# States of batches 2 and 3 turned by TensorE products instead of a transposing transfer, with a new order of the head

## The chip, the cores and the metric

The kernel runs on 1 core of one Trainium2 chip. The metric is device time in microseconds of one execution; times of several runs are given by their median. A profiled execution carries its own time and the span of its instructions.

## The reference

Eight batches of eight heads: a cross attention between 512 tokens `x` and 32 state rows of each head, in both directions, then a two-layer network with a leaky relu over all 8 x 544 rows.

```python
B, H, S, Ns, D = (8, 8, 512, 32, 64)
scores = scale * np.matmul(x, state.transpose(0, 1, 3, 2))     # softmax over the 32 states
xread = np.matmul(a, state)
scores2 = scale * np.matmul(state, x.transpose(0, 1, 3, 2))    # softmax over the 512 tokens
sread = np.matmul(a2, x)
attn = np.concatenate([xread, sread], axis=2)                  # [B, H, 544, 64]
...
h = x @ w_in          # x: attn as [4352, 512]; w_in [512, 2048]
g = np.maximum(0.01 * h, h)
return (g @ w_out)    # w_out [2048, 512]
```

## The kernel before, in words

**Work on a batch.** The kernel never forms `xread`. For each batch it multiplies the scaled states with the rows of `w_in` of their head (`a_m`, L383 to L397), which gives `M`, 256 rows (8 heads x 32 states, as two groups of 128) by 2048; the first layer is then `M` times the probabilities `aT` (`ff1`, L410, for batch 0 `Quad`, L1035), and ScalarE applies the leaky relu on the way out of PSUM (`hT`). The second layer multiplies `hT` with `w_out`: for batch 0 plainly (`piece`), for the others with seven products in place of eight on halves (`Fast`, `Batch`), whose sums of operands VectorE and GpSimd make. The scores (`a_scores`, L221) are products of the states with the transposed x (`xT`). Softmax over states runs on VectorE with 32x32 block operations: `a_top` (`mrow`, L235), `a_rows` (`mrowb`, L243), `a_less` (`sh`, L248), `a_exp` on ScalarE (L255), `a_probs` (L260 to L274, ends in `aT`). The softmax over tokens is `a_max2` (`mcol`, L307) and two exponentials on ScalarE (`a_exp2`, L313).

**What states need.** As left operand of both products a state must stand with D on the partitions: `st_of` (L214) gives 64 rows by 32 columns of a head. For batches 0 and 1 `state01` (L157) makes this: one load of 128 rows of 1 KB (`st0f`, partition p holds four rows of state), a scaling to bf16 (L864), eight products of its 64-column pieces with columns of an identity (L161), and two copies out of PSUM that put the four rows back into order (L165, L169). For batches 2 and 3, and for 4 to 7, `load_state` (L177) makes eight loads into 32 partitions each, `state_t` (L186) scales on GpSimd (L187) and issues a transposing transfer on the SP queue (L188) from `stb` to `st_t`.

**Order.** Every engine's order is written out by hand: the program calls the helpers one after the other, and each engine runs its own calls in that order. Names of the first stretch, the head: `spin` are products without use that keep TensorE going while x loads; `x0_t` transposes batch 0's x on TensorE, `xt0_evict` copies it out; `scores0`/`max0` give the maxima of batch 0 in two halves u of the tokens; `rows0` puts the scores in rows; `split0` splits the negated maximum into two bf16 parts `hi`, `lo`, which `spread0` adds to the scores by products; `exp0`, `sum0`, `recip0`, `probs0` finish the softmax. Loads of weights are issued by GpSimd, x of batch 0 by SP and ScalarE. Batch 1's products (`ff`), batch 2's `M` and scores and the pieces of batch 0's second layer are then mixed by hand, up to a `stretch` of batch 2 whose order is a string, `FIRST`; batches 3 on use `ORDER`. The memset at L1088 touches two columns of `stf`, so that the loads of batches 2 and 3 (SP, L181) come no earlier than it. PSUM is shared by tags: `sc` holds one tile, in turn the scores and some of the `pm` tiles; `ph` and `py` hold two each; `big` one.

Of the kernel before, what the change touches and what calls it, by code (L numbers as in the profile page):

```python
# [9 lines left out]
P = 128  # L10
B, H, S, D = 8, 8, 512, 64
# [19 lines left out]
def kernel(  # L31
# [41 lines left out]
    idle = consts.tile([P, S], BF16, name="idle")  # L73
    nc.vector.memset(idle[:], 0.0)
# [57 lines left out]
    def load_w_out(c, parts=1):  # L132
        n = 4 // parts
        for j in range(4 * c, 4 * (c + 1), n):
            nc.gpsimd.dma_start(
                w_out_bf[:, j:j + n, :],
                moe_w_out[P * j:P * (j + n), :].rearrange("(j p) f -> p j f", p=P),
            )

    def spin(n, tag):  # L140
        p = psum.tile([P, S], FP32, name="pspin", tag=tag, bufs=2 if tag in ("ph", "py") else 1)
        for _ in range(n):
            nc.tensor.matmul(p[:], lhsT=idle[:, :P], rhs=idle[:], start=True, stop=True)
# [30 lines left out]
    stf = [consts.tile([P, hi - lo, P], FP32, name=f"stf{lo}", tag=f"stf{lo}") for lo, hi in groups]  # L174
    stb = [consts.tile([P, hi - lo, P], BF16, name=f"stb{lo}") for lo, hi in groups]
# [689 lines left out]
    spin(7, "py")  # L865
    state01()
    spin(3, "py")


    pxt = {}  # L870

    def x0_t(u, k):
        b = k // 3
        if (u, b) not in pxt:
            pxt[u, b] = psum.tile([P, 3 - 2 * b, 2, P], BF16, name="pxth", tag=("ph", "py")[u])
        for v in range(2):
            nc.tensor.transpose(
                pxt[u, b][:, k % 3, v, :],
                a0.xb[:, 2 * u + v, 2 * k:2 * k + 2, :].rearrange("p h d -> p (h d)"), ident[:],
            )  # L880
# [31 lines left out]
    def spread0(dst, parts, start):  # L912
        for i, part in enumerate(parts):
            for q in range(2):
                for v in range(2):
                    for c in range(NK):
                        n = H * v + NK * q + c
                        nc.tensor.matmul(
                            dst[NS * c:NS * (c + 1), q, P * v:P * (v + 1)],
                            lhsT=part[:, n:n + 1].to_broadcast([P, NS]),  # L920
                            rhs=ident[:], start=start, stop=start or (q == v == i == 1),
                        )
# [8 lines left out]

    def split0(m, eng):
        hi = att.tile([P, NG], BF16, name="hi0", tag="hi0")
        VEC(hi[:], m[:])
        lo = att.tile([P, NG], BF16, name="lo0", tag="lo0")
        with nc.allow_low_precision(reason="the second of two parts of one fp32 value"):
            eng.tensor_tensor(out=lo[:], in0=m[:], in1=hi[:], op=ALU.subtract)
        return hi, lo
# [19 lines left out]
    def recip0(u):  # L958
        q = att.tile([P, NG], BF16, name="q0", tag="q0")
        with nc.allow_low_precision(reason="one rounding, of the finished reciprocal"):  # L960
            nc.vector.reciprocal(q[:], r0[u][:])
        return q

    def recip0_rows(u, q):
        qb0[u] = psum.tile([P, 2, HT], FP32, name="qb0", tag="ph")
        spread0(qb0[u], (q,), True)
# [6 lines left out]
    for c in range(3):  # L973
        load_w_in(c)
    cast_x0(0, 0, NT, VEC)
    for k in (1, 2):
        cast_x0(k, 0, 2, VEC)
    for k in (1, 2):
        cast_x0(k, 2, NT, VEC)
    cast_x0(3, 0, 2, VEC)  # L980
    cast_x0(3, 2, NT, POO)
    for u, k in ((0, 0), (1, 0), (0, 1), (0, 2), (1, 1), (1, 2), (0, 3), (1, 3)):
        x0_t(u, k)
    for u in range(2):
        xt0_evict(u, 0, SCA)
        xt0_evict(u, 1, VEC)
# [3 lines left out]
    for v in range(2):  # L990
        scores0(0, v)
        max0(0, v)
    m = split0(m0[0], nc.gpsimd)
    load_w_in(3)
    load_w_out(0)
    for u in range(2):
        nc.gpsimd.dma_start(
            a1.xb[:, NK * u:NK * (u + 1)].rearrange("p h t d -> p h (t d)"),
            x[1, NK * u:NK * (u + 1)].rearrange("h (p t) d -> p h (t d)", t=NT),
        )  # L1000
    load_w_out(1, 2)
    load_w_out(2)
    for h in (0, NK):
        load_x(2, nc.gpsimd, h, h + NK)
    load_w_out(3, 2)
    rows0(0)
    scores0(1, 0)
    max0(1, 0)
    rows0(1)
    spread0(scn[0], m, False)  # L1010
    exp0(0)
    scores0(1, 1)
    max0(1, 1)
    for u in range(2):
        eps0(u)
    pm = a_m(a0, 0, "big")
    SCA(a0.M[:, 0, :DM], pm[:, 0, :])
    sum0(0)
    m = split0(m0[1], nc.vector)
    q = recip0(0)  # L1020
    spread0(scn[1], m, False)
    exp0(1)
    recip0_rows(0, q)
    VEC(a0.M[:, 1, :DM], pm[:, 1, :])
    probs0(0)
    pm1 = a_m(a1, 0, "sc")
    sum0(1)
    q = recip0(1)
    pm = a_m(a0, 1, "big")
    for g in range(2):  # L1030
        SCA(a0.M[:, g, DM:2 * DM], pm[:, g, :])
# [33 lines left out]
    def m0_evict(c, pm):  # L1065
        for d in range(DM * c, DM * (c + 1), 2 * P):
            VEC(a0.M[:, :, d:d + 2 * P], pm[:, :, d - DM * c:d - DM * c + 2 * P])

    first = Quad(0, 0, "py")
    first.product(range(2))  # L1070
    recip0_rows(1, q)
    probs0(1)
    m_evict(a1, 0, pm1, VEC)
    first.product(range(2, 4))
    first.relu()
    for u, j, tag in (
        (0, 4, "ph"), (1, 0, "big"), (1, 4, "py"), (0, 8, "ph"), (1, 8, "py"), (0, 12, "ph"), (1, 12, "big"),
    ):
        quad = Quad(u, j, tag)
        quad.product()  # L1080
        quad.relu()
        if (u, j) == (1, 0):
            m0_evict(2, a_m(a0, 2, "sc"))
        if (u, j) == (0, 8):
            pm = a_m(a0, 3, "big")
            a_scores(a0)
            m0_evict(3, pm)
            nc.vector.memset(stf[0][:, 0, D - 1:D + 1], 0.0)  # L1088
            a_max2(a0)
# [12 lines left out]
    def m_make(a, c, tag):  # L1102
        pmt[a.b, c] = a_m(a, c, tag)
# [10 lines left out]
    piece(0, h0, 1, 0)  # L1114
    piece(0, h0, 0, 0)
    a_exp2(a0, 0)
    turn(0)
    open_xb(2)
    weights_open()
    wide = psum.tile([P, 2, DM], FP32, name="pyw", tag="big", bufs=1)  # L1120
    VEC(a1.xT[:, :, 0:2, :], pt[0][:])
    turn(1)
    a_exp2(a0, 1)
    piece(0, h0, 2, 0, bank=wide[:, 0])
    VEC(a1.xT[:, :, 2:4, :], pt[1][:])
    load_state(0)
    m_make(a1, 1, "ph")
    a_scores(a1)
    piece(0, h0, 2, 1, copy=None, part=(0, 1))
    m_take(a1, 1, 0, SCA)  # L1130
    piece(0, h0, 0, 1, copy=None, part=(0, 1))
    piece(0, h0, 3, 0, bank=wide[:, 1])
    piece(0, h0, 2, 1, copy=None, part=(2, 3))
    weights_sum(0, 0, 4, nc.gpsimd)
    m_make(a1, 2, "ph")
    piece(0, h0, 3, 1, copy=None, part=(0, 1))
    piece(0, h0, 1, 1, copy=None, part=(0, 1))
    weights_sum(2, 0, 4, nc.gpsimd)
    a_open(a2, 2)
    m_take(a1, 1, 1, VEC)  # L1140
    m_take(a1, 2, 0, SCA)
    piece(0, h0, 3, 1, copy=None, part=(2, 3))
    piece(0, h0, 3, 2, copy=None, part=(0, 1))
    piece(0, h0, 2, 2, copy=None, part=(0, 1))
    a_top(a1)
    state_t(0)
    a_rows(a1)
    a_less(a1)
    a_exp(a1)
    m_take(a1, 2, 1, SCA)  # L1150
    cast_x(2, 0, 4, SCA)
    cast_x(2, 4, 5, POO)
    cast_x(2, 5, 6, POO)
    cast_x(2, 6, 7, POO)
    a_max2(a1)
    a_probs(a1, 0)
    a_probs(a1, 1)
    cast_x(2, 7, 8, POO)
    weights_sum(2, 4, 8)
    a_xt_dma(a2, slice(1, 2))  # L1160
    weights_sum(1, 4, 8)
    weights_sum(3, 4, 8, nc.gpsimd)
    a_exp2(a1, 0)
    weights_sum(1, 0, 4, nc.gpsimd)
    weights_sum(0, 4, 8, nc.gpsimd)
# [3 lines left out]
    piece(0, h0, 2, 2, copy=None, part=(2, 3))  # L1169
    piece(0, h0, 0, 1, copy=None, part=(2, 3))  # L1170
    cast_x(3, 0, 2, POO)
    a_exp2(a1, 1)
    piece(0, h0, 3, 2, copy=None, part=(2, 3))
    piece(0, h0, 0, 2, copy=None, part=(0, 1))
    piece(0, h0, 1, 1, copy=None, part=(2, 3))
    piece(0, h0, 1, 2, copy=None, part=(0, 1))
    piece(0, h0, 1, 2, copy=None, part=(2, 3))
    piece(0, h0, 0, 2, copy=None, part=(2, 3))
    m_make(a1, 3, "ph")
    cast_x(3, 2, 4, POO)  # L1180
    m_take(a1, 3, 0, SCA)
    m_make(a2, 0, "sc")
    m_take(a1, 3, 1, SCA)
    piece(0, h0, 3, 3, copy=None, part=(0, 1))
    ff(0)
    m_take(a2, 0, 0, SCA)
    relu.pop(0)()
    piece(0, h0, 2, 3, copy=None, part=(0, 1))
    piece(0, h0, 3, 3, copy=None, part=(2, 3))
    ff(1)  # L1190
    relu.pop(1)()
    piece(0, h0, 0, 3, copy=None, part=(0, 1))
    piece(0, h0, 2, 3, copy=None, part=(2, 3))
    ff(2)
    m_take(a2, 0, 1, VEC)
    cast_x(3, 4, 6, POO)
    ff(3)
    a_scores(a2)
    y_store(0, 2, VEC)
    a_top(a2)  # L1200
    a_a2t(a0)
    a_rows(a2)
    relu.pop(2)()
    relu.pop(3)()
    y_store(0, 3, SCA)
    ff(4)
    cast_x(3, 6, 8, POO)
    relu.pop(4)()
    piece(0, h0, 0, 3, copy=None, part=(2, 3))
    ff(5)  # L1210
    ff(6, "big")
    a_open(att_of[3], 3)
    a_less(a2)
    piece(0, h0, 1, 3, copy=None, part=(0, 1))
    ff(8)
    y_store(0, 0, SCA)
    relu.pop(5)()
    relu.pop(6)()
    a_max2(a2)
    piece(0, h0, 1, 3, copy=None, part=(2, 3))  # L1220
    y_store(0, 1, VEC)
    before.run(1)
    ff(10, "big")
    relu.pop(8)()
    a_exp(a2)
    a_xt_dma(att_of[3])
    load_state(1, range(0, 2))
    a_a2t(a1)
# [349 lines left out]
```

## Time and profile before

| What | Value |
|---|---|
| median of 3 runs | 201.35 us (201.06 to 201.36) |
| the profiled execution, its own time | 201.61 us |
| its span | 199.8 us |
| granted TensorE clock, mean | 0.998 |
| TensorE / VectorE / ScalarE / GpSimd busy | 193.8 / 164.8 / 150.1 / 63.9 us |
| transposing transfer of the states of batches 2 and 3, issue to landing | 4.4 us |

The table is read against the span: an engine whose busy time is near it has little to give, and what matters is where that engine waits. The profile's rows give starts in us from the span's start. PE is TensorE's products, PEld its weight loads, DVE is VectorE, ACT ScalarE, POOL GpSimd, SP SyncE, which here only issues transfers.

### The profile page before, as it was taken

The page shows a single profiled execution, that of the slowest core. Times are in us where ns is not written, and L with a number is a line of the kernel's source. Part 1 is how long each engine was busy: PE and PEld are TensorE (multiplying, and loading weights), DVE is VectorE, ACT ScalarE, POOL GpSimd, SP SyncE. Part 2 cuts the span into 40 slices and gives each one's busy share as a digit, 9 for nine tenths or more (in the row PEclk, how much of TensorE's full clock was granted, in tenths as well). Part 3 has the DMA queues.
Part 4 walks back from the last instruction along what each step waited for, and adds up shares of the span by engine and source line. Part 5 has one row for each costly group of instructions (what it writes and reads, how often), then busy time and mean ns, then how long its engine had stood idle before and what let it go on. Part 6 is the DMA issues. An engine that isn't in the chain of part 4 may idle for free.

```text
span 199.8 us, 5151 instructions
## 1 busy us (share of the span) xinstructions
PE 193.8 (97%) x2106; PEld 136.5 (68%) x2106; DVE 164.8 (82%) x282; ACT 150.1 (75%) x286; POOL 63.9 (32%) x90
## 2 busy tenths in 40 slices
PE   7999998999999999999999999999999999999993
PEld 2566533446677667767777777777777788799882
DVE  2676498599999998997999899999899877995613
ACT  3478628599779649997899779996999768767710
POOL 8473284790009102720413040500050024005350
PEclk9999999999999999999999999999999999999999
DMA  6999997999571998398293614080013401310026
GB/s 203 212 207 192 199 292 136 206 318 162 101 220 27 197 276 165 58 255 268 51 259 113 184 22 85 3 262 0 3 51 159 82 3 76 134 56 0 5 82 182
DMA packets 40616, 27.50 MB, mean 138 GB/s; under 512 B 25424, under 2 KB 37840, under 8 KB 40592
## 3 DMA queue, kind: packets, MB, share of 16 engines
q1 hardware_dynamic: 34032, 20.35, 39.7%
q0 software_dynamic: 5728, 6.03, 16.8%
q10 hardware_dynamic: 832, 0.79, 1.2%
q8 instruction: 16, 0.26, 0.6%
q14 instruction: 8, 0.07, 0.1%
HBM read 17.30 MB, written 8.91 MB: 131 GB/s over the span
## 4 chain that ended last, share of the span: by engine, by line
PE 90%; DMA 4%; DVE 3%; POOL 0%; issue 0%; ACT 0%; ACTq 0%
PE yq L770 43%; PE ph L414 18%; PE pm L393 4%; PE pf L492 3%; PE yu L770 3%; PE pl L660 3%; PE ph L1051 3%; DMA st_t<-stb 2%; DMA xf<-in_x_dram 2%; PE py L699 2%; PE pl L581 2%; PE pyw L699 1%; PE psn L359 1%; PE sc L225 1%; PE php L1051 1%; PE phw L427 1%
## 5 line engine op out<-in xcount | busy, mean ns | idle before, releaser
L420 ACT ACTIVATE hT<-ph 128x512 bf16<-128x512 f32 x84 | 49.1, 608 | 14.3 <-PE ph L414 14.3
L770 PEld LDWEIGHTS <-su 128*128 128x128 bf16 x480 | 46.2, 98 | 12.4 <-ACT hT L420 0.4
L414 PE MATMUL ph<-aT,M 128*128 128x512 bf16 x168 | 47.9, 379 | 0.0
L770 PEld LDWEIGHTS <-hT 128*128 128x128 bf16 x336 | 32.3, 98 | 12.0 <-issue 2.7
L770 PE MATMUL yq<-tw_xf,su 128*128 128x256 bf16 x224 | 30.8, 273 | 0.0
L770 PE MATMUL yq<-w_out_bf,hT 128*128 128x256 bf16 x224 | 29.2, 273 | 0.0
L114 POOL CAST xb<-xl 128x512 bf16<-128x512 f32 (+1 forms) x24 | 15.2, 673 | 20.9 <-DMA xl<-in_x_dram 20.9
L414 PEld LDWEIGHTS <-M 128*128 128x128 bf16 x168 | 16.0, 98 | 7.7 <-issue 1.9
L759 DVE TENSOR_TENSOR su<-hT 128x1024 bf16<-128x1024 bf16 x28 | 19.1, 686 | 2.6 <-ACT hT L420 2.5
L842 POOL TENSOR_TENSOR yo<-sv,sv 128x512 f32<-128x512 f32 x7 | 9.3, 1330 | 37.2 <-ACT e L313 31.4
L1283 ACT CAST M<-pm 128x512 bf16<-128x512 f32 x30 | 16.8, 596 | 0.6 <-PE pm L393 0.6
L779 ACT COPY sv<-yq 128x512 f32<-128x512 f32 x24 | 14.0, 587 | 3.4 <-PE yq L770 3.3
L770 PE MATMUL yq<-tw_x,su 128*128 128x256 bf16 x112 | 16.3, 273 | 0.0
L770 PE MATMUL yq<-w_out_bf,su 128*128 128x256 bf16 x112 | 15.3, 273 | 0.0
L782 DVE TENSOR_TENSOR yo<-yq,sv 128x512 f32<-128x512 f32 x20 | 13.5, 677 | 2.1 <-PE yq L770 2.1
L770 PE MATMUL yq<-tw_x,hT 128*128 128x256 bf16 x104 | 13.9, 273 | 0.0
L313 ACT ACTIVATE e<-sc,mcol 128x512 bf16<-128x512 f32 x16 | 11.2, 704 | 0.2 <-DVE mcol L307 0.2
L699 PEld LDWEIGHTS <-hT 128*128 128x128 bf16 x64 | 5.9, 98 | 7.4 <-issue 0.9
L759 DVE TENSOR_TENSOR su<-su,hT 128x1024 bf16<-128x1024 bf16 x14 | 10.6, 755 | 0.2
L672 ACT COPY ls<-pl 128x512 f32<-128x512 f32 x16 | 9.5, 592 | 1.5 <-PE pl L660 1.0
L307 DVE TENSOR_REDUCE mcol<-sc 128x2 f32<-128x1024 f32 x8 | 9.7, 1216 | 0.0
L235 DVE TRANSPOSE_TENSOR_REDUCE mrow<-sc 128x32 f32<-128x1024 f32 x7 | 8.7, 1243 | 0.5 <-PE sc L225 0.5
(193 smaller groups left out, 350.8 us busy)
## 6 DMA issues: line engine op xcount, KB each, us to landing
xl<-in_x_dram SPq DMA_DIRECT2D x5, 1024.0 KB, 6.6
out_dram<-yo SPq DMA_DIRECT2D x10, 512.0 KB, 2.9
w_in_bf<-in_moe_w_in_dram POOLq DMA_DIRECT2D x4, 512.0 KB, 7.9
out_dram<-yo SPq DMA_DIRECT2D x7, 256.0 KB, 2.7
w_out_bf<-in_moe_w_out_dram POOLq DMA_DIRECT2D x2, 512.0 KB, 12.8
w_out_bf<-in_moe_w_out_dram POOLq DMA_DIRECT2D x4, 256.0 KB, 13.1
xl<-in_x_dram POOLq DMA_DIRECT2D x2, 512.0 KB, 15.4
out_dram<-ysb SPq DMA_DIRECT2D x4, 256.0 KB, 4.0
```

The lines of the kernel that those rows point to most:

```text
L114: copy(xs[b][:, h0 // NK, :, h0 % NK:h0 % NK + h1 - h0].rearrange("p t h d -> p h t d"), xl[b][:, h0:h1].rearrange("p h (t d) -> p h t d", ...
L307: nc.vector.tensor_reduce(out=a.m2[:], in_=a.sc[:], axis=AX.X, op=ALU.max, negate=True)
L313: nc.scalar.activation(out=a.e2[:, g], in_=a.sc[:, g, :], func=AF.Exp, bias=a.m2[:, g:g + 1], accum_out=a.r2[:, g:g + 1],)
L414: nc.tensor.matmul(ph[:], lhsT=a.M[:, g, P * j:P * (j + 1)], rhs=a.aT[:, g, :], start=(g == 0), stop=(g == 1),)
L420: nc.scalar.activation(out=hT[:, j, :], in_=ph[:], func=AF.Prelu, scale=1.0 / SCALE, alpha=0.01)
L672: copy(self.sv[n], flat)
L699: nc.tensor.matmul(y.py, lhsT=hT[:, j, P * i:P * (i + 1)], rhs=w_out_bf[:, j, :], start=(j == 0), stop=(j == 15),)
L759: (eng or nc.vector).tensor_tensor(out=S[n][:, ms], in0=u[:, ms], in1=v[:, ms], op=op)
L770: nc.tensor.matmul(bank[:, i, :], lhsT=lhs[:, m, P * i:P * (i + 1)], rhs=rhs[:, m, :], start=(first and m == 0 and (i == 0 or of is not No ...
L779: copy(t[:], bank)
L782: nc.vector.tensor_tensor(out=dst, in0=bank, in1=self.sv[n][:], op=ALU.add)
L1283: copy(t.M[:, g, DM * c:DM * (c + 1)], src[g][:] if isinstance(src, list) else src[:, g, :])
```

## The change

1. **States of batches 2 and 3.** One load of 128 rows of 1 KB on the SP queue takes the place of the eight; it is issued early, behind a memset that now stands on GpSimd after the first three weight loads. VectorE scales it in the head between two maxima of batch 0, TensorE turns it by eight products with identity columns (64 columns wide) into a tile of tag `sc`, and ScalarE copies it to `st_t`. The eight loads, GpSimd's scaling and the transposing transfer of this pair go. Batches 4 to 7 keep theirs.
2. **Spins** take their operands from a constant 1.0, so the idle tile and its memset go; they are 8 + 1 in place of 7 + 3, the last one between two groups of transposes.
3. **Order.** `split0` and other helpers are cut into single calls, and the order of the head, of the mixed part and of `FIRST` is written anew. In the mixed part the first `M` product of batch 2 comes ahead of the last of batch 1, four copies of `M` stand in a row on ScalarE, and two copies of batch 1's third chunk are VectorE's.

```diff
-    idle = consts.tile([P, S], BF16, name="idle")
-    nc.vector.memset(idle[:], 0.0)
...
+    def ones_at(n):
+        return nc.const_aps.tensor(1.0, (P, n), BF16)
...
-            nc.tensor.matmul(p[:], lhsT=idle[:, :P], rhs=idle[:], start=True, stop=True)
+            nc.tensor.matmul(p[:], lhsT=ones_at(P), rhs=ones_at(S), start=True, stop=True)
...
+    def load_state23():
+        nc.sync.dma_start(
+            stf[0][:], state[2:4].rearrange("b h n d -> (b h n) d").rearrange("(p r) d -> p r d", r=4)
+        )
+
+    def scale_state23(eng):
+        if eng is nc.scalar:
+            eng.mul(stb[0][:], stf[0][:], SCALE)
+        else:
+            eng.tensor_scalar(out=stb[0][:], in0=stf[0][:], scalar1=SCALE, scalar2=None, op0=ALU.mult)
+
+    def place_state23(tag):
+        ps = psum.tile([P, 4, D], FP32, name="pst2", tag=tag, bufs=1)
+        for r in range(4):
+            for g in range(2):
+                nc.tensor.matmul(
+                    ps[D * g:D * (g + 1), r, :], lhsT=stb[0][:, r, :], rhs=heads[:, :, :, g],
+                    start=True, stop=True,
+                )
+        pst.append(ps)
+
+    def take_state23(copy):
+        copy(
+            st_t[0][:].rearrange("p b (k q r) -> p (b k) q r", k=NK, r=4),
+            pst[0][:].rearrange("p r (h q) -> p h q r", q=8),
+        )
...
-    spin(7, "py")
+    spin(8, "py")
     state01()
-    spin(3, "py")
...
-            nc.vector.memset(stf[0][:, 0, D - 1:D + 1], 0.0)
...
+    load_w_in(2)
+    nc.gpsimd.memset(stf[0][:, 0, D - 2:D], 0.0)
+    load_state23()
...
+    max0(1, 0)
+    scale_state23(nc.vector)
+    rows0(1)
...
+    max0(1, 1)
+    eps0(0)
+    eps0(1)
+    m0_make(0, "big")
+    m0_half(0, 0, SCA)
+    sum0(0)
+    place_state23("sc")
+    take_state23(SCA)
+    hi0(1)
+    lo0(1, nc.vector)
+    recip0(0)
+    spread0(scn[1], hi[1], False, False)
+    spread0(scn[1], lo[1], False)
+    exp0(1)
...
-    load_state(0)
...
-    state_t(0)
...
+    a_less(a1)
+    a_exp(a1)
+    piece(0, h0, 1, 2, copy=None, part=(0, 1))
+    m_take(a1, 2, 0, VEC)
+    m_take(a1, 2, 1, VEC)
+    a_max2(a1)
...
+    a_exp2(a1, 1)
+    m_make(a2, 0, "sc")
+    cast_x(3, 2, 4, POO)
+    m_make(a1, 3, "ph")
+    piece(0, h0, 0, 3, copy=None, part=(0, 1))
+    piece(0, h0, 3, 3, copy=None, part=(0, 1))
+    cast_x(3, 4, 6, POO)
+    piece(0, h0, 2, 3, copy=None, part=(0, 1))
+    ff(0)
+    m_take(a1, 3, 0, SCA)
+    m_take(a1, 3, 1, SCA)
+    m_take(a2, 0, 0, SCA)
+    m_take(a2, 0, 1, SCA)
...
```

Three places of the new order follow. The first is VectorE's queue in the head, from the split of the first half's maximum to the first reciprocal (`m` the maxima, `hi`/`lo` the split, `stb`/`stf` the states). Before:

```order
L934 CAST hi_208<-m_200 128x16
L927 TENSOR_REDUCE m_238<-sct 128x8 x2
L934 CAST hi_310<-m_238 128x16
L937 TENSOR_TENSOR lo_312<-m_238,hi_310 128x16
L961 RECIPROCAL q_314<-r_289 128x16
```

The same place after the change:

```order
L962 TENSOR_REDUCE m_239<-sct 128x8
L195 TENSOR_SCALAR stb_128<-stf_126 128x256
L962 TENSOR_REDUCE m_239<-sct 128x8
L1006 CAST hi_322<-m_239 128x16
L1011 TENSOR_TENSOR lo_324<-m_239,hi_322 128x16
L988 RECIPROCAL q_326<-r_291 128x16
```

The scaling of the new states stands between the two maxima of the second half, and the split and the reciprocal stand behind it.

The second place is VectorE's queue in the middle, in batch 1's softmax (`sh` to `aT`, `mcol` the maximum over tokens). Before:

```order
L248 TENSOR_TENSOR sh<-sc,mrowb 128x1024
L307 TENSOR_REDUCE mcol<-sc 128x2
L260 TENSOR_REDUCE r_683<-e_674 128x32
L264 TENSOR_SCALAR r_683<-r_683 128x32
L267 RECIPROCAL qh<-r_683 128x32
L273 STREAM_TRANSPOSE qb<-qh 128x512
L274 TENSOR_TENSOR aT<-e_674,qb 128x1024
```

After:

```order
L284 TENSOR_TENSOR sh<-sc,mrowb 128x1024
L1083 CAST M<-pm 128x512 x2
L343 TENSOR_REDUCE mcol<-sc 128x2
L296 TENSOR_REDUCE r_688<-e_678 128x32
L300 TENSOR_SCALAR r_688<-r_688 128x32
L303 RECIPROCAL qh<-r_688 128x32
L309 STREAM_TRANSPOSE qb<-qh 128x512
L310 TENSOR_TENSOR aT<-e_678,qb 128x1024
```

Two copies of `M` have come in between `sh` and `mcol`.

The third place is the start of the SP queue, the transfers that SP issues. Before:

```order
L69 DMA xf<-in_x_dram 128x2x256 x2
L181 DMA stf_128<-in_state_dram 32x2x64 x8
L188 DMA_TRANSPOSE st_t_123<-stb_130 128x2x128
L209 DMA_TRANSPOSE xT<-xb 128x8x128 x2
L108 DMA xl<-in_x_dram 128x8x256
```

After:

```order
L69 DMA xf<-in_x_dram 128x2x256 x2
L187 DMA stf_126<-in_state_dram 128x256
L245 DMA_TRANSPOSE xT<-xb 128x8x128 x2
L106 DMA xl<-in_x_dram 128x8x256
L751 DMA out_dram<-ysb 128x512
```

One load stands for eight, and no transpose of states is queued ahead of that of x.

More of the change, by code (lines that the diff above doesn't have):

```diff
@@ L930, in max0 @@
         )
[L932 to L938, printed above, removed]
     def exp0(u):
@@ L971, in probs0 @@
         )
[L973 to L986, printed above, removed]
     a0.aT = att.tile([P, 2, S], BF16, name="aT", tag="aT")
```

381 lines of the change are left out of this document (207 added, 174 removed), and 14 rows, old and new, of the table FIRST.

## The prediction

> **What bounds the kernel now.** I read the page first: the busy shares of its part 1 and the chain of its part 4.
>
> ```profile
> PE 193.8 (97%) x2106; PEld 136.5 (68%) x2106; DVE 164.8 (82%) x282; ACT 150.1 (75%) x286; POOL 63.9 (32%) x90
> PE 90%; DMA 4%; DVE 3%; POOL 0%; issue 0%; ACT 0%; ACTq 0%
> ```
>
> TensorE (PE) is busy for 97% of the span and makes up 90% of the chain that ends last. So the change is worth what it takes from PE's own work and from PE's waits, and it costs what it adds to them. The view of waits, asked for PE alone, has three entries for the whole kernel (engine and line, what was waited for: us in all, times, longest).
>
> ```profile
> PE pspin L143 <- DVE warm L76: 1.2, 1, 1.2
> PE pm L393 <- DMA st_t<-stb: 1.0, 1, 1.0
> PE pxth L877 <- DVE xb L121: 0.2, 1, 0.2
> ```
>
> The first and third lie ahead of 6 us, under the load of x. The second is the one that the change can remove: the first product of batch 2 (`pm` from `st_t`) waits 1.0 us for the transposing transfer. From there to the end PE waits for nothing, so the middle can give 1.0 us and no more. Two stretches must be walked: the head, where the new work is put, and the middle, where the wait is.
>
> **The head: what is added.** Rows of the timeline (start us, busy us, engine, line, operation, in brackets idle time before it and what ended it).
>
> ```profile
> 3.07 2.50 POOL L127 DMA_DIRECT2D w_in_bf<-in_moe_w_in_dram  x3
> 3.54 0.55 DVE L864 TENSOR_SCALAR stb<-st0f 128x256 bf16<-128x256 f32 x1 [2.41 <-DMA st0f<-in_state_dram]
> 4.28 0.40 PE L161 MATMUL pst<-identg,stb 128*64 128x96 bf16 x8
> 4.72 0.37 ACT L165 CAST stbd<-pst 128x256 bf16<-128x256 f32 x1 [1.04 <-PE pst L161]
> 8.42 0.42 DVE L927 TENSOR_REDUCE m<-sct 128x8 f32<-128x256 f32 x1
> 9.54 0.42 DVE L927 TENSOR_REDUCE m<-sct 128x8 f32<-128x256 f32 x1 [0.70 <-PE sct L892]
> 9.98 0.25 PE L953 MATMUL r<-ones,e 128*128 128x4 bf16 x4
> 10.00 0.30 DVE L934 CAST hi<-m 128x16 bf16<-128x16 f32 x1
> 10.35 0.41 PE L918 MATMUL scn<-ident,hi 128*32 128x128 bf16 x16
> 11.03 0.60 ACT L942 ACTIVATE e<-scn 128x512 bf16<-128x512 f32 x1 [0.45 <-PE scn L918]
> ```
>
> Four things are added. Batches 0 and 1 already go the same way, so each has a row of the same shape: the scaling 0.55 us on VectorE (DVE, the L864 row), eight products 0.40 us (L161, 96 columns wide where the new ones have 64), the copy out of PSUM 0.37 us on ScalarE (ACT, L165), and the load.
>
> The scaling is put between the two maxima of the second half of batch 0, the rows at 8.42 and 9.54. DVE sits idle there for 0.70 us, so 0.55 us fit, if the load has landed by about 8.9. If it has not, the scaling holds DVE's queue. Behind it stand the maximum of 9.54, the split (`hi` at 10.00), the first reciprocal and the copy of `M`; for `hi` PE waits at 10.35, and for that sum the exponential at 11.03. PE's eight new products also stand in order ahead of the products with `hi`. After these rows the head has no idle time that could take up a delay: PE reaches the rest of the program later by the same amount.
>
> So the landing decides. The load waits for a small memset that now stands on GpSimd (POOL) behind the issue of three weight loads, which ends at 3.07 + 2.50 = 5.57. In the kernel before, the state's loads went out 0.10 us after their memset's start (next fence, 19.52 to 19.62); with one more tenth for the memset itself the issue is at about 5.75. From issue to landing the list of transfers has two rows of this tensor (count, KB each, median us to landing; the 16-KB loads are those of batches 2 and 3).
>
> ```profile
> stf<-in_state_dram SPq DMA_DIRECT2D x8, 16.0 KB, 5.0
> st0f<-in_state_dram ACTq DMA_DIRECT2D x1, 128.0 KB, 2.8
> ```
>
> And the timeline at that place:
>
> ```profile
> 19.52 0.06 DVE L1088 MEMSET stf<- 128x2 f32 x1
> 19.62 3.63 SPq L181 DMA_DIRECT2D stf<-in_state_dram  x8
> ```
>
> The row of the same size and shape, `st0f`, took 2.8 us, but it was issued at 0.72, when nothing else was under way. The eight `stf` loads took 5.0 us each (4.9 to 5.2), though each has an eighth of the bytes; they ran beside the weight loads of POOL's queue. The view by stretches shows which state of the DMA engines the new load meets (last columns: TensorE clock, mean busy share of the 16 engines, GB/s).
>
> ```profile
> 5.75:8.75 3.00, 2.82 (x54) 1.66 (x56) 2.54 (x11) 1.50 (x2) 0.61 (x2) 1.00 1.22 199
> 19.50:24.50 5.00, 5.00 (x60) 3.21 (x57) 2.23 (x5) 3.93 (x9) 1.42 (x2) 1.00 1.33 199
> ```
>
> 199 GB/s in both, busy share 1.22 and 1.33: the engines are full after 5.75 exactly as they were when a state load took 5.0 us. The ends are therefore a landing at 5.75 + 2.8 = 8.55, which costs nothing, and, if the larger load behaves like all eight small ones together (first issue 19.62, last issue 19.62 + 3.63 - 0.42, landing 5.2 later, in all about 8.4 us), one at about 14.1. I take the row it is nearest to, same queue and same load beside it: 5.75 + 4.95 = 10.7.
>
> DVE then scales until 11.25 and takes the maximum at about 11.3 in place of 9.54: the head is late by **1.75 us**. The products (0.40) run beside that maximum and the split, and the copy (0.37) ends ahead of the exponential, now at 12.8, so both cost nothing. That cover is gone if the load is in time: PE has then 10.35 - (9.98 + 0.25) = 0.12 us idle, and the products cost 0.40 - 0.12 = 0.3 us.
>
> The Trainium skill, DMA: Bandwidth & Descriptors, section Anatomy of one DMA, gives (for loads from GpSimd) 2.0 us plus bytes over 436 GB/s, an estimate of 2.3 us for 128 KB and 2.0 us for 16 KB; by it the load lands at 8.05 and the sum would be the first rival's. The 2.8 of `st0f` is near that, the 5.0 of `stf` is not. The same page, section Latency and other measured facts, has HBM answering in 0.2 us on average and in 2 us at high load; 1.8 us more than `st0f`'s row would land the state at about 10.35, for a sum 0.35 us smaller than mine.
>
> Fewer spin products (9 for 10), the order of the spins, and the idle tile's memset that goes lie ahead of the x casts for which PE waits anyway: nothing, either way at most the 0.2 us of that wait. The new load's 128 KB at 199 GB/s push the weights behind it by up to 0.65 us; PE waited for no weight in the list above, and with a late head it has more room. Nothing is taken, 0.3 us is kept in the range.
>
> **The middle: what is removed.**
>
> ```profile
> 29.63 1.21 DVE L307 TENSOR_REDUCE mcol<-sc 128x2 f32<-128x1024 f32 x1
> 30.66 1.27 SPq L188 DMA_TRANSPOSE st_t<-stb  x1
> 32.12 0.69 ACT L313 ACTIVATE e<-sc,mcol 128x512 bf16<-128x512 f32 x1
> 32.79 0.68 ACT L313 ACTIVATE e<-sc,mcol 128x512 bf16<-128x512 f32 x1
> 33.46 0.88 DVE L274 TENSOR_TENSOR aT<-e,qb 128x1024 bf16<-128x1024 bf16 x1
> 33.70 0.41 PE L393 MATMUL pm<-w_in_bf,st 64*32 64x512 bf16 x8
> 34.18 1.07 ACT L1107 CAST M<-pm 128x512 bf16<-128x512 f32 x2 [0.61 <-PE pm L393]
> 35.07 0.41 PE L393 MATMUL pm<-w_in_bf,st_t 64*32 64x512 bf16 x8 [0.96 <-DMA st_t<-stb]
> 36.30 0.69 DVE L1107 CAST M<-pm 128x512 bf16<-128x512 f32 x1
> 36.49 0.60 ACT L420 ACTIVATE hT<-ph 128x512 bf16<-128x512 f32 x1 [0.29 <-PE ph L414]
> 39.40 0.41 PE L225 MATMUL sc<-xT,st_t 64*32 64x512 bf16 x8
> ```
>
> The chain of waits has the price of two products of 512 columns, 0.43 us:
>
> ```profile
> 38.18 0.43 PE pyw L699 x2
> ```
>
> I count to the scores of batch 2 (39.40): both kernels have done the same products by then. The wait ahead of 35.07 goes: **-1.0 us**. What is late next, in the old clock:
>
> - The product of batch 2 now stands ahead of that of batch 1 and uses the PSUM bank of batch 1's scores, which the second exponential (32.79 + 0.68 = 33.47) must leave. DVE has two casts of `M` (2 x 0.69 = 1.38) more ahead of `mcol`, so `mcol` ends at 29.63 + 1.21 + 1.38 = 32.22 and the two exponentials (1.35 together) near 33.6. PE arrives at 33.70: a wait of up to 0.1.
> - Softmax of batch 1 (`aT`, end 34.34) slides by the same 1.38 to 35.7. Its first user comes behind both `pm` groups (from 33.7, 0.41 each, end 34.5) and six products of 0.215 each, at 35.8: a tie.
> - ACT has four casts of `M` in a row: from 34.6 at 0.535 each to 36.7, then activations to 37.3 and 37.85. The third and fourth product of the layer need the banks that these free, and come at 37.5 and 37.9: a tie again.
>
> I take 0.1 us for the three together: the scores come at 38.5, -0.9 us. The transposed x that they read could stand in the way.
>
> ```profile
> L209 SPq DMA_TRANSPOSE xT<-xb x2: 1232/1262/1291, 33.8 to 35.2; - x2
> DMA to landing us min/median/max: 3.2/3.4/3.6
> ```
>
> It lands at 35.15 + 3.6 = 38.8 or earlier, since it no longer shares the queue with `st_t`. With a late head PE comes at 40.2 and this costs nothing; with a punctual one it comes at 38.8, a tie.
>
> POOL loses a scaling and SP eight issues and one transpose, all off the path. Behind 39.40 both kernels do the same work on PE without waits, so the difference stays.
>
> **Sum.** +1.75 - 0.9 = **+0.85 us**. The profiled execution took 201.61 (span 199.8 and 1.8 around it), so it would be 202.5; the median of the runs shown is 201.35, 0.26 below it, which gives 202.2 for the median.
>
> **Rivals.**
>
> 1. *The load is in time* (2.8 us as `st0f`, or anything up to 3.2): no wait on DVE, 0.3 us for the products, -0.9 in the middle: -0.6, so 200.75; 200.35 if the products find room too. For it: the 1-KB rows and the fitting DVE gap. Against it: the full engines. It is the case on the other side, and it decides as the landing moves: each us later than 8.9 is a us of head, and beyond about 9.8 the change loses.
> 2. *Half-way landing*, 9.4 to 10.2: within 0.4 us of no change, about 201.35. HBM that is merely slow to answer would give it.
> 3. *The removed wait is replaced in its place* by one for ACT: the bank of the scores is left late, since everything there ties. The 1.0 us comes back, and the change does not do what it says: 201.35 + 1.75 = 203.1 with a late load, 201.65 with a punctual one.
>
> **How the numbers follow.** A measurement of this kernel can tell about 0.2%, 0.4 us. My forecast has 0.52 (all slower). Rival 1 has 0.26: 0.24 faster, 0.02 within. Rival 2 has 0.12, within. Rival 3 has 0.10: 0.07 slower, 0.03 within. Together faster 0.24, same 0.17, slower 0.59. Cases of both signs hold weight, so the range reaches from rival 1 with room for its better end (200.6) to a landing near 11.7 or rival 3 (203.2); the forecast's own range, landings of 10.3 to 11.3, is 201.8 to 202.8.
>
> **What would show it.** In the changed profile: DVE's scaling of `stf` (L195) with an idle time of almost 2 us before it, released by the state's load, starting near 10.7; the load 5 us from issue to landing; PE's products with `hi` near 12.1; no PE wait for `st_t`; batch 2's scores near 40.2. I am wrong if that scaling starts before 9.4, if PE waits for ACT or DVE ahead of the first product of batch 2, or if some later wait shows on PE.

## The result, and the profile after

The changed kernel takes **204.49 us** (median of 6 executions, 202.57 to 205.64), the kernel before 201.28 beside it: ratio 1.014, 95% interval 1.009 to 1.019. The ratio compares fast executions only and so leaves out the slowest one, of 205.64 us, which had a mean clock of 0.980. It is slower, and it lies above the predicted range. The profiled execution took 203.91 (span 202.1), 2.30 us more than the one of before.

The view of waits of the changed kernel, TensorE's entries:

```profile
PE pst L201 <- DVE m L962: 1.6, 1, 1.6
PE pspin L150 <- PEq L1638: 0.8, 1, 0.8
PE ph L450 <- issue: 0.5, 3, 0.2
PE pxth L913 <- DVE xb L119: 0.3, 1, 0.3
```

The wait for `st_t` is gone and a new one of 1.6 us stands in the head, at the first product that turns the new states (`pst`). The timeline of VectorE in the changed kernel shows where it comes from:

```profile
11.53 0.29 DVE L195 TENSOR_SCALAR stb<-stf 128x256 bf16<-128x256 f32 x1 [2.28 <-DMA stf<-in_state_dram]
11.73 0.42 DVE L962 TENSOR_REDUCE m<-sct 128x8 f32<-128x256 f32 x1
12.19 0.17 DVE L1006 CAST hi<-m 128x16 bf16<-128x16 f32 x1
```

The scaling sat idle for 2.28 us until the load landed, as predicted, and the maximum behind it starts at 11.73 instead of 9.54. The list of that line gives the load's own time (issue, and from issue to landing):

```profile
L187 SPq DMA_DIRECT2D stf<-in_state_dram x1: 341/341/341, 5.7 to 5.7; - x1
DMA to landing us min/median/max: 5.7/5.7/5.7
```

Now TensorE's timeline at the same place. Compare the products with `hi` (L953, 0.62 us) with the same sixteen products in the row of 10.35 that the prediction shows (0.41 us).

```profile
10.39 0.25 PE L980 MATMUL r<-ones,e 128*128 128x4 bf16 x4
12.20 0.33 PE L201 MATMUL pst<-ident,stb 128*64 128x64 bf16 x8 [1.56 <-DVE m L962]
12.47 0.62 PE L953 MATMUL scn<-ident,hi 128*32 128x128 bf16 x16
13.87 0.63 PE L429 MATMUL pm<-w_in_bf,st 64*32 64x512 bf16 x8
15.19 0.89 PE L1031 MATMUL ph<-aT,M 128*128 128x256 bf16 x4
```

They are slower because the clock is. The view by stretches has the granted TensorE clock in its last columns (clock, DMA share, GB/s); first before, then after:

```profile
10.50:12.00 1.50, 1.36 (x68) 0.92 (x60) 1.47 (x5) 0.68 (x2) 1.50 (x3) 1.00 1.23 203
12.00:14.00 2.00, 2.00 (x36) 1.34 (x29) 0.95 (x3) 1.65 (x4) 1.93 (x3) 1.00 1.25 208
14.00:16.00 2.00, 2.00 (x24) 1.40 (x22) 1.20 (x2) 1.86 (x4) 0.76 (x1) 1.00 1.25 204
```

```profile
10.50:12.00 1.50, 0.14 (x4) 0.15 (x3) 0.47 (x2) 0.49 (x1) 1.50 (x3) 1.00 1.24 211
12.00:14.00 2.00, 1.80 (x64) 1.52 (x63) 1.22 (x6) 0.81 (x2) 2.00 (x4) 0.59 1.24 209
14.00:16.00 2.00, 2.00 (x24) 0.75 (x17) 0.94 (x2) 0.83 (x3) 0.63 (x2) 0.55 1.25 206
16.00:18.00 2.00, 2.00 (x32) 1.69 (x32) 1.47 (x2) 1.92 (x5) 0.46 (x2) 1.00 1.24 206
```

In the stretch of the wait PE is busy for 0.14 of 1.5 us; from 12.4 to 15.8 us, 3.41 us by the clock's own records, it then has half clock. TensorE was not idle in those 3.41 us, its work only went more slowly.

The scores of batch 2, at 39.40 before:

```profile
41.49 0.41 PE L261 MATMUL sc<-xT,st_t 64*32 64x512 bf16 x8
```

Starts of the same products on TensorE, read from the timelines of before and of each run, as differences from before in us:

| product | before | after | e1 | e2 | e3 | e4 | e5 | e6 | e7 |
|---|---|---|---|---|---|---|---|---|---|
| `hi`, second half | 10.35 | +2.11 | +2.45 | +0.06 | +0.31 | +2.96 | +0.81 | +0.84 | +0.05 |
| first product of the layer (L1051, after: L1031) | 12.21 | +2.97 | +2.45 | +0.09 | +0.31 | +3.82 | +0.81 | +0.84 | +0.05 |
| scores, batch 1 | 25.02 | +3.24 | +2.45 | +0.09 | +0.44 | +5.24 | +0.81 | +0.84 | +0.05 |
| scores, batch 2 | 39.40 | +2.09 | +1.29 | -0.66 | -0.71 | +4.19 | +0.54 | -0.21 | +0.47 |
| scores, batch 4 | 92.73 | +2.28 | +1.50 | -0.39 | -0.80 | +4.39 | +0.52 | -0.05 | +0.94 |
| last (`yz`) | 195.51 | +2.28 | +1.50 | +0.40 | -0.80 | +4.40 | +0.52 | -0.05 | +0.94 |

After: 2.11 by the late states, 1.13 more until the clock is back, -1.15 in the middle, 0.19 further on.

### The profile page after: what moved, and what is told of

The parts are those of the page before. It is cut to its first block, busy times and chain, and to the rows that moved or that the text cites. A ratio compares the mean times of both kernels' runs of the same rounds, so it can differ in the third digit from the quotient of the medians.

```text
span 202.1 us, 5129 instructions
## 1 busy us (share of the span) xinstructions
PE 194.2 (96%) x2091; PEld 137.6 (68%) x2113; DVE 164.7 (82%) x283; ACT 149.4 (74%) x285; POOL 61.4 (30%) x90
## 4 chain that ended last, share of the span: by engine, by line
PE 84%; DVE 7%; DMA 3%; POOL 2%; ACT 1%; issue 1%; POOLq 0%; DVEq 0%
PE yq L806 39%; PE ph L450 15%; PE pm L429 4%; PE pyw L735 4%; PE py L735 3%; PE pf L528 3%; PE ph L1031 3%; PE yu L806 3%; DMA stf<-in_state_dram 3%; PE pl L696 3%; PE pl L617 2%; POOL w_in_bf L125 1%; DVE lq L680 1%; DVE su L795 1%; PE sc L261 1%
## 5 line engine op out<-in xcount | busy, mean ns | idle before, releaser
L450 PE MATMUL ph<-aT,M 128*128 128x512 bf16 x149 | 44.3, 379 | 0.8 <-issue 0.5
L112 POOL CAST xb<-xl 128x512 bf16<-128x512 f32 (+1 forms) x24 | 13.5, 600 | 17.1 <-DMA xl<-in_x_dram 17.1
L1359 ACT CAST M<-pm 128x512 bf16<-128x512 f32 x31 | 17.4, 596 | 0.7 <-PE pm L429 0.6
L815 ACT COPY sv<-yq 128x512 f32<-128x512 f32 x23 | 13.3, 585 | 2.6 <-PE yq L806 2.5
L291 ACT ACTIVATE e<-sh 128x1024 bf16<-128x1024 f32 x7 | 7.4, 1058 | 3.8 <-DVE sh L284 3.8
L795 DVE TENSOR_TENSOR su<-su,hT 128x1024 bf16<-128x1024 bf16 x14 | 9.6, 687 | 0.3
```

What stands on the lines that cost most here:

```text
L112: copy(xs[b][:, h0 // NK, :, h0 % NK:h0 % NK + h1 - h0].rearrange("p t h d -> p h t d"), xl[b][:, h0:h1].rearrange("p h (t d) -> p h t d", ...
L450: nc.tensor.matmul(ph[:], lhsT=a.M[:, g, P * j:P * (j + 1)], rhs=a.aT[:, g, :], start=(g == 0), stop=(g == 1),)
L795: (eng or nc.vector).tensor_tensor(out=S[n][:, ms], in0=u[:, ms], in1=v[:, ms], op=op)
L815: copy(t[:], bank)
L1359: copy(t.M[:, g, DM * c:DM * (c + 1)], src[g][:] if isinstance(src, list) else src[:, g, :])
```

## The experiments

My theory after the result: the late load costs the head 2.1 us of waiting, this wait in its turn takes the clock, and the middle gains what the wait for `st_t` was. The rivals: the slow head belongs to the new order or to the load's own traffic; the gain in the middle belongs to the order.

**e1, the wait kept busy.** The changed kernel with 15 products of zeros (0.12 us each), added to a bank in front of the turning products.

```diff
+    for _ in range(15):
+        nc.tensor.matmul(scn[1][:NS, 0, :], lhsT=zeros[:, :NS], rhs=zeros[:], start=False, stop=False)
     place_state23("sc")
```

> The changed kernel with one addition: in TensorE's wait for the scaled states (10.6 to 12.2 us) it runs 15 products of zeros, 256 columns each, into the open sum of the second half's scores, which adds nothing. Vector engine's wait for the load stays as it is. Theory (the wait costs twice: about 1.7 us itself, and then a stretch of 3.4 us at half the granted clock, worth about 1.1 us or more): the granted clock stays at 1.00 after 12 us, the products with hi still come near 12.4, the first product of the network comes about 1.1 us earlier than in the changed kernel (near 14.1 for 15.2), and the time is 202.3 to 203 us. Rival (the new order as such costs the time, the clock is a by-product): no change from the changed kernel, 203.5 to 205.

Measured: 203.29 us, ratio 1.008 (1.005 to 1.011). In this execution the load took 6.1 us, so the head's wait is no shorter (+2.45 at `hi`), but it grows no further:

```profile
12.80 0.41 PE L955 MATMUL scn<-ident,hi 128*32 128x128 bf16 x16
14.66 0.61 PE L1033 MATMUL ph<-aT,M 128*128 128x256 bf16 x4
```

```profile
12.00:14.00 2.00, 1.44 (x64) 1.10 (x64) 1.86 (x7) 0.89 (x2) 1.90 (x3) 1.00 1.25 208
14.00:16.00 2.00, 1.86 (x37) 1.23 (x38) 0.92 (x3) 1.28 (x4) 0.56 (x1) 1.00 1.24 206
```

The clock stays at 1.00 and the sixteen products take 0.41 us. So an idle TensorE, not the load, takes the clock; products without use give back 1.2 us of the median. The time lies 0.3 us above the 203 at which my expectation ended, since the load was later than in the changed kernel.

**e2, the states used late.** The load stays, the scaling goes behind batch 1's first copy of `M`, the turning products and the copy go to about 32 us.

```diff
-    scale_state23(nc.vector)
     rows0(1)
...
-    place_state23("sc")
-    take_state23(SCA)
...
     m_evict(a1, 0, pmt[1, 0], VEC)
+    scale_state23(nc.vector)
...
+    place_state23("ph")
     cast_x(2, 0, 4, SCA)
+    take_state23(SCA)
```

> The changed kernel, the load issued at the same place, but its use put off: Vector engine scales behind the copy of batch 1's first M chunk (near 15.5 us), the eight products and the copy out stand near 32 us in a PSUM bank that is free there. Theory (all of the loss is the wait for the load and its clock; the middle gains 1.0): no wait in the head, clock 1.00 throughout, scores of batch 2 near 38.7 for 39.4 in the kernel before, time 0.4 to 0.9 us below the kernel before. Rival 1 (the new order costs on its own): still 1 us or more above the kernel before. Rival 2 (the load takes bandwidth from x and the weights): TensorE waits for weights, or x lands 0.2 to 0.6 us later, and the time is within 0.4 us of the kernel before.

Measured: 201.93 us, ratio 1.001 (0.999 to 1.003). The load still takes 5.8 us and nobody waits for it; the head is that of before. The time I expected, 0.4 to 0.9 us below before, did not come. The gain at batch 2 (0.66 us) is there in the profile and is lost again, 0.35 us between 77 and 84 us and 0.8 near 187; how, is told under e8.

**e3, the load early.** Its gate goes ahead of the first weight load instead of behind the third.

```diff
+    nc.gpsimd.memset(stf[0][:, 0, D - 2:D], 0.0)
     load_w_in(0)
     load_w_in(1)
     load_w_in(2)
-    nc.gpsimd.memset(stf[0][:, 0, D - 2:D], 0.0)
```

> The changed kernel with the memset that gates the load moved ahead of the first weight load, so that SP issues the load at about 3.2 us; uses stay in their places. Theory (the load took 5.7 us because it was issued into full weight queues, at 5.7): it lands by 8.5, Vector engine does not wait for it, clock 1.00, and the time is 0.2 to 0.7 us below the kernel before (1.0 gained in the middle, 0.3 for the products, up to 0.4 if x lands later). Rival (a state load takes 5 us and more whatever is beside it): landing at 8.9 or later, half of the wait stays, time 0.5 us or more above the kernel before.

Measured: 201.05 us, ratio 0.999 (0.997 to 1.001); the profiled execution 200.82, clock 0.999.

```profile
L187 SPq DMA_DIRECT2D stf<-in_state_dram x1: 341/341/341, 3.3 to 3.3; - x1
DMA to landing us min/median/max: 3.5/3.5/3.5
```

Ahead of the weights the same load takes 3.5 us, lands at 6.8, and nobody waits for it. The second half's `hi` is 0.31 us late in this execution, but the first half's, ahead of all that the change adds on TensorE, is already 0.25 late (8.82 for 8.57), as are VectorE's casts of x, which end at 6.82 for 6.58; the turning products add 0.06 us. At the last product the profiled execution is 0.80 us ahead of before. The median is 0.44 us below the 201.49 of the kernel before beside it, as I expected (0.2 to 0.7), but the interval of the ratio holds 1, so a gain is not shown. This is the prediction's first rival (-0.6 us), made to happen.

**e4, e5, e6, a delay without the change.** The kernel before, with nine, three or five memsets (0.39 us apart) on VectorE ahead of the second half's maximum: no new load, no new order.

```diff
     scores0(1, 1)
+    for _ in range(9):
+        nc.vector.memset(idle[:], 0.0)
     max0(1, 1)
```

> The kernel before, with nine useless memsets of the idle tile (0.27 us each) on Vector engine ahead of the last maximum of batch 0, that is at the place where the changed kernel scales the states: Vector engine is 2.4 us busy where it had 0.7 idle, a delay of about 1.7 us, with no transfer in it. Theory: TensorE idles 1.8 us near 10.4, the clock falls to half afterwards for about 3.4 us in most executions, and the time rises by 2.5 to 3.5 us, more than the delay. Rival (the clock fell for another reason in the changed kernel, its spins of ones or its order): clock 1.00, time up by 1.7 us.

> The kernel before with three memsets (0.39 us apart) on the vector engine ahead of the maximum of unit 1, which then starts near 10.4 us instead of 9.54: a delay of 0.85 us in the head, with no transfer in it. Theory of the clock (a wait that is long enough in this thin stretch takes the matrix engine to half clock; 0.85 us is too short): the granted clock stays at 1.0 from 12 to 16 us, the marks of the head stand 0.6 to 0.9 us later and no more, the wait for the turned states in the middle swallows most of it, and the time is 201.3 to 201.7 us. Rival (every delay in the head is paid more than once over): the head's last marks stand 1.4 us later, 202.0 us or more.

> The same with five memsets: the maximum starts near 11.2 us, a delay of 1.65 us, about that of the changed kernel (11.73 us), in the order of before and without its load. Theory of the clock: the wait is long enough, the granted clock falls to 0.5 for 3.4 us from about 12.4 us, the first scores stand 2.7 to 3.2 us later; the wait in the middle gives 1.0 back; 203.1 to 203.5 us. Rival (the loss of clock belongs to the new order or to the load): the clock stays at 1.0, the first scores stand 1.6 us later, 201.9 to 202.2 us.

Measured: e4 204.79 us (ratio 1.015, 1.011 to 1.018), e5 201.63 (1.001, 1.000 to 1.002), e6 202.09 (1.004, 1.002 to 1.007). The delays were not the ones meant. In e4 the maximum came at 12.68, 3.1 us late, and a weight load that landed late had added to the wait before it. In e5 and e6 it came at 10.54 and 10.57, 1.0 us late: the memsets begin in the 0.7 us in which VectorE is idle anyway, which I had forgotten, and in e5 the scores of the first half came 0.7 us late besides. The time of e4 lies in the range that I had expected (2.5 to 3.5 us more), but by luck, since its delay was almost twice the one meant. The stretches and waits of e4:

```profile
12.00:14.00 2.00, 0.69 (x28) 0.69 (x32) 1.71 (x7) 0.18 (x1) 1.78 (x4) 0.61 1.24 209
14.00:16.00 2.00, 2.00 (x52) 0.94 (x40) 1.12 (x3) 0.60 (x1) 0.66 (x1) 0.50 1.26 204
16.00:18.00 2.00, 2.00 (x31) 1.12 (x24) 0.26 (x1) 1.57 (x3) 0.75 (x1) 0.50 1.22 201
```

```profile
PE scn L918 <- DVE hi L934: 1.6, 1, 1.6
PE pm L393 <- DMA w_in_bf<-in_moe_w_in_dram: 1.0, 1, 1.0
```

Without the change, waits of 1.0 and 1.6 us close together halve the clock, here for 6.8 us: the loss needs neither the new order nor the new load. In e6 the wait is shorter:

```profile
PE scn L918 <- DVE hi L934: 1.0, 1, 1.0
```

The profiled execution of e6 kept its clock, so my expectation for it fell (203.1 to 203.5 us); the median is the rival's (201.9 to 202.2), though with a shorter delay than either assumed. 3 of its 10 executions have a mean clock of 0.992 or less, and they took 202.57 to 203.58. With e5's wait (0.2 us) none of 10 has that, and its time is the expected one; in e4 all 4 do, with the changed kernel's 1.56 us 5 of 6, and the sixth, at clock 1.000, took 202.57. So the loss of the clock is a matter of chance that grows with the wait, as far as the wait of the one profiled execution stands for the others. A low mean clock does not say where it was lost: of 87 executions of the kernel before beside the experiments two have 0.992 or less, and one of e8 has 0.988 at 201.79 us.

What the chance is, the clock's own records suggest. In every trace the stretches of one clock between the first and the last border last a multiple of 3.41 us (after the change 6.83 at full, 3.41 at half, 187.73 at full), so the clock changes only at borders 3.41 us apart. Between such borders, PE's busy time and then the clock, first after the change, then in e6:

```profile
8.96:12.37 3.41, 1.79 (x64) 1.00 1.22 219
12.37:15.79 3.42, 3.42 (x79) 0.50 1.24 207
```

```profile
8.50:11.91 3.41, 2.37 (x104) 1.00 1.24 207
11.91:15.33 3.42, 3.28 (x65) 1.00 1.24 207
```

The piece ahead of the loss holds 1.79 us of work after the change (1.66 in e4), and the clock stayed after one with 2.37. The borders lie elsewhere in each execution, and so may cut a wait in two or not. That this decides the executions without a trace is argued, not shown.

**e7, the old load in the new order.**

```diff
-    load_state23()
...
     piece(0, h0, 2, 0, bank=wide[:, 0])
+    load_state(0)
...
     weights_sum(0, 0, 4, nc.gpsimd)
+    state_t(0)
```

> The changed kernel in its new order, with the states of batches 2 and 3 loaded as before (eight transfers of 256-byte runs near 19 us, scaled on GpSimd behind two weight sums, turned by a transposing transfer). It tells the new order from the new load. Theory (the order as such is worth 0.1 to 0.2 us, the 1.0 us in the middle is the transfer's): no wait for the states in the head, no half clock, marks up to the first scores within 0.2 us of before; the wait for the turned states is back at 0.8 to 1.2 us, the scores of batch 2 stand within 0.2 us of before, and the time is 201.1 to 201.5 us. Rival (the order brings the gain by itself): the scores of batch 2 stand 0.7 us or more ahead of before with the old load, 200.5 us.

Measured: 201.73 us, ratio 1.002 (1.001 to 1.003).

```profile
PE pm L429 <- DMA st_t<-stb: 1.5, 1, 1.5
```

The wait is back, and longer (1.5 for 1.0 us), since the new order asks for `st_t` 0.28 us earlier and the transfer lands 0.26 us later. The gain in the middle is the load's; the order with the old load loses 0.4 us there. Wait and time are both above what I expected (0.8 to 1.2 us, 201.1 to 201.5). The 1.5 us of waiting did not touch the clock: all 12 executions have 0.997 or more. Two things differ from the head. Around this wait stand full products of 512 columns, in the head small ones; and in the profiled execution a border at 34.45 us cuts the wait in two, which leaves more work in each piece:

```profile
31.04:34.45 3.41, 2.79 (x13) 1.00 0.76 132
34.45:37.87 3.42, 2.49 (x25) 1.00 0.82 150
```

No run separates the two.

**e8, e9, e10, a search for what the later part takes.** e3's and e2's later parts differ, by traces. Where e2 loses 0.8 us, near 187 us, VectorE and GpSimd both add tiles in SBUF. First e2, then e3:

```profile
187.59 1.27 POOL L878 TENSOR_TENSOR yo<-sv,sv 128x512 f32<-128x512 f32 x1 [3.35 <-issue]
```

```profile
187.62 1.79 DVE L795 TENSOR_TENSOR su<-hs,su 128x1024 bf16<-128x1024 bf16 x1
```

```profile
187.19 1.82 POOL L878 TENSOR_TENSOR yo<-sv,sv 128x512 f32<-128x512 f32 x1 [3.36 <-issue]
```

```profile
187.20 0.68 DVE L795 TENSOR_TENSOR su<-hs,su 128x1024 bf16<-128x1024 bf16 x1
```

One of the two is longer by most of the other's duration: they take turns. Where VectorE loses, TensorE waits (0.6 us in e2). e8 is e3 with GpSimd's addition moved to VectorE behind the next join; e9 moves that of batch 1 (near 64 us) as well; e10 is e9 with e2's late use.

```diff
-            elif n == 7:
-                nc.gpsimd.tensor_tensor(...)
+            elif n == 7 and self.b < B - 1:
+                self.add7(nc.vector if self.b == 1 else nc.gpsimd)
...
             fs.join(ysb[0][:, :, :HC], bank, 1)
+            before.add7(nc.vector)
+            before.out(1, slice(HC, DM))
```

> The early load of e3, and the last addition of batch 7 on GpSimd (128x512, 1.27 us, which starts within 0.03 us of a vector addition of 128x1024 near 187 us) moved to the vector engine behind the next join, where it is idle. Theory (the executions differ because those two additions collide, and the one that starts later waits: 1.79 us for the vector addition in the slower profile, 0.68 us in the faster): the executions near 201.6 us and above mostly go, the median is 200.6 to 200.9 us, and the vector addition takes 0.68 us. Rival (the spread has another cause, transfers say): the median stays at 201.0 us with executions on both sides of 201.3.

> e8 with one more addition taken from GpSimd: that of batch 1 (128x512) goes to the vector engine behind the copy that makes its input, ahead of a stretch of 0.7 us in which the vector engine waits for products; it met a vector addition near 63.8 us in the profile of e8 (1.65 us instead of 0.68, and the products behind it wait 0.5 us), and not in that of e3. Theory (the executions of one kernel differ by these meetings of GpSimd and vector additions): no vector addition of 128x1024 takes over 1.2 us near 64 and 187 us, the executions lie within 200.6 to 201.3 us, median 200.8 us, ratio 0.996 to 0.998. Rival (the meetings near 80 us with the casts, or transfers, set the spread): executions up to 201.9 us again and a median of 201.2 us or more.

> e9 with the late turn of e2 besides (scaled behind the copies of batch 1, products and copy near 32 us): early load, late turn, both additions moved. Theory: the products and the copy leave the head, whose marks then stand within 0.1 us of before instead of 0.3 us behind it; the middle and the end are those of e9: 200.5 to 200.8 us, 0.2 us below e9. Rival (the late turn takes its 0.3 us from the middle instead): the same time as e9 within 0.1 us.

Measured: e8 201.45 us (ratio 0.999, 0.998 to 1.001), e9 201.16 (1.000, 0.998 to 1.001), e10 201.35 (1.001, 1.000 to 1.002). All three lie above the ranges that I expected. My theory that these two additions set the spread fell: e9's executions still reach from 200.62 to 201.86. The profiled one is the fastest, 0.99 us ahead of before at its last product. A third meeting place shows when e9 and e10 are compared: four casts of x on GpSimd start when that x has landed, at 75.33 us in e9 and at 76.60 in e10, on top of a chain of additions on VectorE (`lq`, 0.28 us alone). In e9, then in e10:

```profile
75.33 2.42 POOL L112 CAST xb<-xl 128x512 bf16<-128x512 f32 x4 [1.63 <-DMA xl<-in_x_dram]
77.20 0.69 DVE L680 TENSOR_TENSOR lq<-aT,lq 128x256 bf16<-128x256 bf16 x1
77.81 0.28 DVE L680 TENSOR_TENSOR lq<-M,lq 128x256 bf16<-128x256 bf16 x1
78.01 0.28 DVE L680 TENSOR_TENSOR lq<-lq,aT 128x256 bf16<-128x256 bf16 x1
```

```profile
76.60 2.46 POOL L112 CAST xb<-xl 128x512 bf16<-128x512 f32 x4 [2.65 <-DMA xl<-in_x_dram]
77.28 0.69 DVE L680 TENSOR_TENSOR lq<-aT,lq 128x256 bf16<-128x256 bf16 x1
77.89 0.69 DVE L680 TENSOR_TENSOR lq<-M,lq 128x256 bf16<-128x256 bf16 x1
78.50 0.69 DVE L680 TENSOR_TENSOR lq<-lq,aT 128x256 bf16<-128x256 bf16 x1
```

In e10 the three additions shown all meet a cast, in e9 one of three does, and PE is 0.6 us further behind e9 at 87 us than at 74. So in these profiles the landing of x decides by 0.6 us. I did not move those casts; that they explain the whole spread is argued, not shown.

**e11, the gate one place later than e3's**, behind one weight load.

```diff
     load_w_in(0)
+    nc.gpsimd.memset(stf[0][:, 0, D - 2:D], 0.0)
     load_w_in(1)
     load_w_in(2)
-    nc.gpsimd.memset(stf[0][:, 0, D - 2:D], 0.0)
```

> The changed kernel with the gate of its state load one place behind the first weight load instead of behind the third. Issued at 3.32 us (e3) the load landed after 3.5 us, at 5.72 us (the changed kernel) after 5.7 us. Theory (what lies ahead of it on the shared transfer engines sets the landing): issued near 4.1 us it lands after 4.0 to 4.6 us, near 8.4 us, ahead of the vector engine's turn at 9.5 us; no wait in the head, the clock stays at 1.0, and the time is that of e3, 200.8 to 201.4 us. Rival (behind any weight load it takes 5 us or more): it lands past 9.5 us, and the head waits again for what it is past that.

Measured: 201.19 us, ratio 1.000 (0.998 to 1.003).

```profile
L187 SPq DMA_DIRECT2D stf<-in_state_dram x1: 341/341/341, 4.2 to 4.2; - x1
DMA to landing us min/median/max: 5.2/5.2/5.2
```

My 4.0 to 4.6 us fell, and the rival's "5 us behind any weight load" held: one weight load ahead costs 1.7 us (5.2 for 3.5), two more cost 0.5 (5.7). It lands near 9.4, ahead of the 9.5 that the rival had named: the scaling waits 0.63 us for it, the maximum comes at 9.68, 0.14 us late, and the time is in the range that I expected.

## Why the prediction was wrong, step by step

- **Issue at 5.75**: 5.72. Right.
- **Landing 5.0 us later**: 5.7, in e1 and e2 6.1 and 5.8. The row chosen was the right one of the two (5.0, not `st0f`'s 2.8), the size 0.7 us short.
- **Scaling 0.55 us**: 0.29 us; the landing's 0.7 less this 0.26 makes the maximum 0.43 later than predicted, 11.73 for 11.3.
- **"The products (0.40) run beside that maximum and the split"**: wrong. The tile `pst2` has the tag `sc`, and that bank held the second half's `sct`, which the maximum reads. The profile names the releaser itself: `pst` waited for `m`, not for `stb`. The products therefore run only from 12.20 to 12.47, ahead of the products with `hi`. The price is small all the same: `hi` itself was split by 12.36, and in the kernel before and in e6 TensorE starts 0.05 to 0.06 us behind that, so they held it up by about 0.05 us. The split's faster cast (0.17 for 0.30 us) gave more than that back. The products with `hi` came at 12.47 instead of "near 12.1" because the maximum came late.
- **The products for a load in time, 0.3 us**: 0.06 us in e3.
- **"PE reaches the rest of the program later by the same amount"**: this step failed. A wait on TensorE was priced at its length. It took the clock with it, and 2.11 us became 3.24. The one execution that kept its clock took 202.57 us, inside the forecast's own range (201.8 to 202.8). In the profile of before the clock stands at 1.00 through the head, and neither a bound nor a rival was kept for a loss, so the range was too short above. A hint was there: in the first row of TensorE a spin product of 512 columns takes 0.45 us (3.17 for seven), twice what a product of 512 columns takes later (0.43 for two), although the column of the clock reads 1.00 there too; the clock's records begin only at 4.4 us.

```profile
1.18 3.17 PE L143 MATMUL pspin<-idle 128*128 128x512 bf16 x7 [1.18 <-DVE warm L76]
```

- **Middle -0.9 us**: -1.15, and the same in e3, so "1.0 us and no more" was too little: the new order gives 0.15 to 0.2 us beside the wait, where, no run separates. The three ties for which 0.1 was taken cost nothing, and no wait appeared in their place: rival 3 did not come true.
- **Sum +0.85 us**: +2.28 in the profile. The terms: 0.36 for the head's wait (2.11 for 1.75), 1.13 for the clock, -0.25 for the middle, 0.19 further on (near 80 us, where two of the `lq` additions take 0.70 and 0.69 us beside GpSimd's casts): 1.43 in all, which is the difference. The median lies 3.2 us above before's; the executions of 205.07 and 205.23 us show the same mean clock as the profiled one of 203.91, and what they lose besides is in no trace. This stays open.
- **Rival 1's better end, 200.35**: by its own terms (-0.9) it is 200.45; and the range, which was to hold it, began at 200.6.

The Trainium skill, TensorE: Matmul & The Clock Gate, Part 1, states that the clock halves after an idle window of about 3.4 us and is full again after a busy window of the same length, and that the windows run freely. The 3.41 us at half clock, and borders that lie elsewhere in each execution, agree. That the window must be idle does not: the one that lost the clock here held 1.79 us of work in 3.41. Its advice (section Why this matters for your kernels) to avoid idle gaps over about 3 us is too generous for this kernel: a wait of 1.56 us in a thin stretch halved the clock in the profiled execution, and 5 of 6 executions have a mean clock of 0.992 or less.

## What to carry to other kernels

A wait on TensorE has two prices, its length and what the clock does after it: where small products stand around it, add a term for a stretch at half clock, or put products without use into the wait. A load's time is read from the row with the same traffic beside it, and the cheap cure is its place in the queue: ahead of the first bulk load, not behind it. Before work is called hidden, follow its PSUM bank to the last reader: a shared tag is a wait, even if it cost little here.

## What the runs showed of the hardware that was not expected

- Half clock came in pieces of 3.41 us (one after the change, two in e4), on borders 3.41 us apart, behind pieces in which TensorE was busy for 1.79 and 1.66 us; it did not come behind pieces with 2.37 us (e6), nor after a wait of 1.5 us among full products (e7).
- A 128-KB load of 1-KB rows took 3.5 us ahead of the weight loads, 5.2 behind one and 5.7 to 6.1 behind three.
- Additions in SBUF on VectorE and GpSimd exclude each other: 0.68 us became 1.79 when GpSimd's began 0.03 us earlier, and GpSimd's 1.27 became 1.82 when VectorE won, with starts 0.01 us apart. The Trainium skill, SBUF — State Buffer, section SBUF: two separate sides, calls it an exclusive lock for the whole instruction; the rows agree.
- No version tried beats the kernel before by more than its measurement can tell; the best medians are e3's 201.05 and e9's 201.16 us.
